# GpSimd's 16-point phases ahead of the third root, their sine in the silu stretch, and a forward slab's tables two places behind its first stage

## The chip, the cores and the metric

The kernel runs on one core of a Trainium2 chip. The metric is device time in microseconds (us) of one execution of the whole program, 204.77 us before the change (median of 3 runs, 204.67 to 204.78). Beside it stands a profile of one further execution. Engines are written as the profile writes them: PE is TensorE's matmul and PEld its weight load, DVE is VectorE, ACT is ScalarE, POOL is GpSimd, SP is SyncE, which issues the DMAs. Every engine works through its own instructions in the order in which the program wrote them.

## The reference

The input x is 2048 rows of 640 elements. It is normalised by row, and then takes two ways: a two-dimensional Fourier filter, and a gated feed-forward network whose output passes a silu. The two are multiplied and added to x.

```python
xn = _layernorm(x, axis=-1)
# spectral part, over both axes of (S, D) = (2048, 640)
X = rfft2(xn)
X = X * (w_r + 1j * w_i)
s = irfft2(X)                                   # to bfloat16
# feed-forward part, F = 1536
g = silu((gelu(xn @ w_gate) * (xn @ w_up)) @ w_down)
return x + s * g
```

## The kernel before

**The two ways.** The feed-forward network is what fills TensorE. It runs over four groups (g) of 512 rows. In a group, for each of twelve tiles of 128 features, a *half* of five matmuls gives the gate (`psg`, then a GELU `ge` on ScalarE) and another half gives the up projection (`psu`, then the product `uT` on VectorE, line 795). Then follow the down projections of the group's four slabs of 128 rows: each slab in three thirds of eight matmuls, in chains of twelve that end in a silu (`G`, line 819, groups 0 and 3) or in a tanh form of it (`th`, `G`, lines 822 and 823, groups 1 and 2). `psg` and `psu` have two PSUM buffers each.

The Fourier filter is done by matmuls with tables of sines that the kernel computes. Its forward part goes over 16 slabs, slab n1 holding the rows with index n1 modulo 16. `slab_S1` (the *first stage*) multiplies five folded chunks of the slab by the table `Tfwd` into `pz` and casts it on ScalarE to `GEN` (line 545; the buffer shares the tile GEN, and there are four such places). `slab_D` (the *tables*: the matmuls with `FT`) takes that cast through six matmuls into `pd`, casts it on ScalarE to `zd` (line 579, four buffers), and SyncE stores it to `ZDR` in two DMAs (line 582). Both stages draw `pz` and `pd` from one ring of two PSUM buffers. When all 16 slabs are stored, `load_B2` reads them back, turned, into B in ten DMAs; a middle part of 16-point transforms (`s2_in`, `s2_out`, tables MG, N1, N2) and an inverse part follow, between the pieces of groups 2 and 3 of the network.

**What is folded.** Ahead of a first stage VectorE normalises a slab (`norm`, line 205) and folds it, four slabs at a time: `fold_x`, `fold_a`, `fold_b` give the chunks f, and `fold_y` in three steps gives the last chunk y. Row statistics come from `stats`; `root` computes the reciprocal standard deviations of four slabs, an addition on VectorE and a power on GpSimd (line 199). The third such root of four, for slabs 8 to 11, is `root, 8, 4`.

**The 16-point tables.** MG is built from the sines of 128 small phases. `mg_iota` and `mg_phase1` prepare constants on GpSimd. `mg_phase2` computes the phases `vg` with eight small GpSimd instructions (line 378). `mg_mask` takes them modulo 2048 on VectorE (line 417). `mg_sin` is their sine on ScalarE (`sg`, line 421), and `mg_build` copies and signs them into MG and MJ on GpSimd. `mg_turn` transposes both by DMA at places 45 and 46. The table sines Tinv and FT are computed at place 22, right behind an instruction that brings in the Silu table.

**What sets the order.** The order is written out by hand. The list `back` holds the pieces of the network. The n-th of them is called *place* n here. Places 0 to 23 are group 0's halves, 24 to 35 its down thirds, 36 to 59 group 1's halves (even places gate, odd places up), 60 to 71 its down thirds. `put(p, ...)` appends a step to place p. The program writes each piece and then the steps put at its place, in the order of the `put` calls. So an item of place p stands behind the piece of place p on every engine that both use. Nothing is moved after that; an engine starts its next instruction when its inputs and buffers are ready.

For the forward slabs the list `FA` names the place of each first stage, and the tables stand one place behind:

```python
    FA = (30, 32, 33, 35, 37, 39, 40, 42, 44, 46, 48, 50, 54, 55, 57, 58)
    for n1 in range(NS):
        put(FA[n1] + 1, slab_D, n1)
        put(FA[n1], slab_S1, n1)
```

Where slab n's tables and slab n+1's first stage share a place, the tables come first. `load_B2` is put at place 60, the first `s2_in` at place 67.

Of the kernel before, what the change touches and what calls it, by code (L numbers as in the profile page):

```python
# [32 lines left out]
def kernel(  # L33
# [40 lines left out]
    with tc.manual_schedule():  # L74
        build(nc, locals())


def build(nc, env):
# [792 lines left out]
    def put(s, *item):  # L871
        plan[s].append(item)
# [22 lines left out]
    put(0, lists)  # L895
    put(13, mg_iota)
    put(13, mg_phase1)
    put(23, mg_phase2)
    for it in ((silu_table,), (tinv_sin, 0), (tinv_sin, 1), (ft_sin, 0)):
        put(22, *it)  # L900
    for q in range(4):
        put(23 + q, tfwd, q)
    put(28, ft_sin, 1)
    put(36, mg_mask)
    put(37, mg_sin)
    put(37, mg_build)
    for at, *items in (
            (17, (stats, 8)), (18, (stats, 9)), (20, (stats, 10)), (22, (stats, 11), (root, 8, 4)),
            (24, (fold_x, 0, 4, 0), (fold_x, 0, 4, 1)), (25, (fold_a, 0, 4, 0), (fold_a, 0, 4, 1)),
            (26, (fold_b, 0, 4, 0), (fold_b, 0, 4, 1)), (27, (fold_y, 0, 4, 0), (fold_y, 0, 4, 1), (fold_y, 0, 4, 2)),  # L910
            (28, (norm, 8)), (29, (fold_x, 4, 4, 0), (fold_x, 4, 4, 1)), (30, (fold_a, 4, 4, 0)),
            (31, (fold_a, 4, 4, 1), (fold_b, 4, 4, 0)), (32, (fold_b, 4, 4, 1), (fold_y, 4, 4, 0)),
            (33, (fold_y, 4, 4, 1), (fold_y, 4, 4, 2), (norm, 9)), (34, (norm, 10), (norm, 11)), (35, (stats, 12)),
            (36, (stats, 13)), (37, (fold_x, 8, 4, 0)), (38, (fold_x, 8, 4, 1), (fold_a, 8, 4, 0)),
            (39, (fold_a, 8, 4, 1)), (40, (fold_b, 8, 4, 0), (fold_b, 8, 4, 1)), (41, (fold_y, 8, 4, 0)),
            (42, (fold_y, 8, 4, 1), (fold_y, 8, 4, 2), (half_stats, 14, 0)), (43, (half_stats, 14, 1)),
            (44, (stats, 15), (root, 12, 4)), (46, (norm, 12), (norm, 13)),
            (47, (norm, 14), (norm, 15)), (48, (fold_x, 12, 4, 0), (fold_x, 12, 4, 1)),
            (49, (fold_a, 12, 4, 0)), (50, (fold_a, 12, 4, 1), (fold_b, 12, 4, 0)), (51, (fold_b, 12, 4, 1)),
            (52, (fold_y, 12, 4, 0), (fold_y, 12, 4, 1)), (53, (fold_y, 12, 4, 2))):  # L920
        for it in items:
            put(at, *it)
    F0 = 30
    TURN = 45
    FA = (30, 32, 33, 35, 37, 39, 40, 42, 44, 46, 48, 50, 54, 55, 57, 58)
    for n1 in range(NS):
        put(FA[n1] + 1, slab_D, n1)
        put(FA[n1], slab_S1, n1)
    z_end = F0 + 30
    for k in range(4):  # L930
# [87 lines left out]
```

## Time and profile before

| what | value |
|---|---|
| median of 3 runs | 204.77 us (204.67 to 204.78) |
| the profiled execution | 204.84 us |
| its span in the trace | 203.1 us |
| PE busy | 195.4 us, 96% of the span |
| DVE busy | 132.0 us, 65% |
| ACT busy | 125.7 us, 62% |
| POOL busy | 37.9 us, 19% |
| DMA, mean over the span | 160 GB/s |
| places 30 to 60, by the trace | 41.7 to 88.7 us |

The span is counted from the first to the last instruction; the execution's own time has 1.7 us around it. An engine's busy time is a union of its instructions as drawn, and the drawn end of a matmul is modelled: consecutive starts tell more than ends. A row of the timeline reads: start in us from the beginning of the span, duration, engine, line of the kernel, operation, out<-in, shapes, and in brackets the idle time before it with what ended it. Consecutive instructions of one kind are merged into one row (x5). A row of the waits reads: who waited, for whom, the sum in us, how often, the longest.

### The profile page before, as it was taken

How to read it: one execution, taken by the hardware profiler on the slowest of the kernel's cores; microseconds unless marked ns; L12 is line 12 of the kernel's file. 1: busy time of each engine (PE TensorE's matmuls, PEld its weight loads, DVE VectorE, ACT ScalarE, POOL GpSimd, SP SyncE). 2: the span in 40 equal slices, each digit the busy share in tenths (PEclk: the TensorE clock that was granted, in tenths of full speed). 3: DMA queues.
4: the chain of work that ended last, by engine and by line, in shares of the span. 5: the costliest groups of instructions: out<-in, count | busy, mean ns of one | idle time of the engine just before them, and what ended most of it. 6: DMA issues, size and time to landing. Idle time of an engine off the chain costs nothing.

```text
span 203.1 us, 4169 instructions
## 1 busy us (share of the span) xinstructions
PE 195.4 (96%) x1549; PEld 118.2 (58%) x1549; DVE 132.0 (65%) x320; ACT 125.7 (62%) x219; POOL 37.9 (19%) x62
## 2 busy tenths in 40 slices
PE   7989999999789999999999999999999999999993
PEld 5778854777345555566643434357765555556773
DVE  7876969799757696222666476433239787878573
ACT  2548657967996665742687778623564756476632
POOL 5427679994050200000000000000000000000000
PEclk9999999999999999999999999999999999999999
DMA  5999999455558628227963222239900507141612
GB/s 168 340 343 329 400 282 177 90 186 194 136 145 143 167 76 325 82 65 219 326 163 67 74 97 97 100 103 269 303 8 2 164 4 221 36 129 39 190 62 70
DMA packets 40325, 32.44 MB, mean 160 GB/s; under 512 B 15088, under 2 KB 38256, under 8 KB 40048
## 3 DMA queue, kind: packets, MB, share of 16 engines
q1 hardware_dynamic: 40304, 32.17, 56.1%
q8 instruction: 12, 0.20, 0.4%
q14 instruction: 9, 0.07, 0.1%
HBM read 19.03 MB, written 7.88 MB: 133 GB/s over the span
## 4 chain that ended last, share of the span: by engine, by line
PE 67%; ACT 1%; issue 1%; DVE 0%
PE psg L789 18%; PE psu L789 17%; PE psg L814 10%; PE psu L814 9%; PE pv L706 2%; PE pd L553 2%; PE pu L653 2%; PE px L626 2%; PE pd L574 2%; PE pz L543 1%; PE pd L557 1%; ACT GEN L545 0%; PE pd L576 0%; ACT G L819 0%; DVE Yall L764 0%
## 5 line engine op out<-in xcount | busy, mean ns | idle before, releaser
L789 PE MATMUL psu<-xnT,Wu 128*128 128x512 bf16 (+2 forms) x295 | 61.5, 339 | 0.5 <-DVE uT L795 0.3
L789 PE MATMUL psg<-xnT,Wg 128*128 128x512 bf16 (+2 forms) x295 | 61.5, 341 | 0.0
L795 DVE TENSOR_TENSOR uT<-psu,ge 128x512 bf16<-128x512 f32 (+2 forms) x59 | 34.4, 587 | 29.4 <-PE psu L789 20.5
L793 ACT ACTIVATE ge<-psg 128x512 bf16<-128x512 f32 (+2 forms) x59 | 30.5, 517 | 26.7 <-PE psg L789 24.8
L814 PEld LDWEIGHTS <-uT 128*128 128x128 bf16 x396 | 37.2, 98 | 14.0 <-issue 0.4
L789 PEld LDWEIGHTS <-Wu 128*128 128x128 bf16 x295 | 26.4, 98 | 22.1 <-issue 3.2
L789 PEld LDWEIGHTS <-Wg 128*128 128x128 bf16 x295 | 26.6, 99 | 20.8 <-issue 1.6
L814 PE MATMUL psg<-Wd,uT 128*128 128x320 bf16 (+1 forms) x204 | 30.5, 294 | 0.0
L814 PE MATMUL psu<-Wd,uT 128*128 128x320 bf16 (+1 forms) x192 | 29.0, 296 | 0.0
L638 DVE TENSOR_TENSOR X<-xs,W 128x972 bf16<-128x972 bf16 (+2 forms) x22 | 13.3, 648 | 10.2 <-ACT xs L634 9.3
L579 ACT CAST zd<-pd 128x660 bf16<-128x660 f32 x16 | 11.3, 708 | 6.0 <-PE pd L576 3.5
L183 DVE BATCH_NORM_STATS2 st<-X 128x6 f32<-128x320 bf16 x32 | 14.1, 479 | 0.3 <-DMA X<-in_A_x_dram 0.2
L708 ACT CAST W<-pv 128x640 bf16<-128x640 f32 x16 | 11.1, 695 | 5.0 <-PE pv L706 5.0
L731 ACT ACTIVATE W<-pd 128x960 bf16<-128x960 f32 (+2 forms) x14 | 10.0, 779 | 5.8 <-PE pd L557 5.5
L659 ACT CAST X<-pu 128x486 bf16<-128x486 f32 (+4 forms) x22 | 12.3, 558 | 0.4
L545 ACT CAST GEN<-pz 128x640 bf16<-128x640 f32 x16 | 11.1, 691 | 1.8 <-PE pz L543 1.8
L634 ACT CAST xs<-px 128x972 bf16<-128x972 f32 (+2 forms) x11 | 10.3, 937 | 2.9 <-PE px L626 2.9
L823 DVE SCALAR_TENSOR_TENSOR G<-th,psg 128x320 bf16<-128x320 f32 x8 | 3.9, 488 | 11.7 <-ACT th L822 11.7
L737 DVE TENSOR_TENSOR W<-W 128x960 bf16<-128x960 bf16 (+1 forms) x12 | 6.9, 598 | 4.1 <-ACT W L731 4.1
L764 DVE TENSOR_TENSOR Yall<-Yall,G 128x640 bf16<-128x640 bf16 (+3 forms) x19 | 8.2, 434 | 1.4 <-ACT G L819 1.1
L574 PE MATMUL pd<-FT,GEN 128*128 128x132 bf16 x64 | 6.6, 227 | 2.4 <-ACT GEN L545 2.2
L574 PEld LDWEIGHTS <-GEN 128*128 128x128 bf16 x64 | 4.0, 98 | 8.2 <-ACT GEN L545 8.0
(135 smaller groups left out, 214.4 us busy)
## 6 DMA issues: line engine op xcount, KB each, us to landing
W<-W SPq DMA_DIRECT2D x4, 642.0 KB, 3.5
ZDR<-zd SPq DMA_DIRECT2D x32, 80.2 KB, 2.6
xt<-in_A_x_dram SPq DMA_DIRECT2D x8, 320.0 KB, 3.7
UDR<-X SPq DMA_DIRECT2D x10, 240.8 KB, 2.5
out_dram<-Yall SPq DMA_DIRECT2D x14, 160.0 KB, 2.2
B<-ZDR SPq DMA_DIRECT2D x8, 240.8 KB, 4.5
W<-UDR SPq DMA_DIRECT2D x4, 481.5 KB, 6.5
X<-in_A_x_dram SPq DMA_DIRECT2D x3, 640.0 KB, 7.2
```

Of the source, the lines that this page charges most:

```text
L183: nc.vector.bn_stats(out=st[:, k, :], in_=X[:, n1, 320 * k:320 * k + 320])
L545: nc.scalar.copy(out=Zt[n1], in_=pz)
L574: nc.tensor.matmul(l_cols(pd[:, g % 2], g), lhsT=z[:, g, :], rhs=FT[:, g, :], start=True, stop=True)
L579: nc.scalar.copy(out=zd.rearrange("p c (q e) -> p c q e", e=10), in_=pd[:, :, 0:330].rearrange("p c (e q) -> p c q e", q=33))
L634: nc.scalar.copy(out=xs, in_=px[:, :, 0:n * w].rearrange("p k (h l) -> p k h l", l=w))
L638: nc.vector.tensor_tensor(out=pp[-1], in0=xs, in1=WT[:, :, h0:h0 + n, l0:l0 + w], op=ALU.mult)
L659: nc.scalar.copy(out=us[:, :, :, c0:c0 + (w + 1 - m) // 2], in_=pv[:, :, :, m:w:2])
L708: nc.scalar.copy(out=vs, in_=pv)
L789: nc.tensor.matmul(ps, lhsT=WT[:, c, t * P:(t + 1) * P], rhs=xnT[g][:, c, c0:c1_], start=(c == 0), stop=(c == 4))
L793: nc.scalar.activation(out=ges[t], in_=ps, func=ACT.Gelu_apprx_tanh)
L795: nc.vector.tensor_tensor(out=uT[g][:, t, c0:c1_], in0=ps, in1=ges[t], op=ALU.mult)
L814: nc.tensor.matmul(ph, lhsT=uT[g][:, t, j * P:(j + 1) * P], rhs=Wd[:, t, c0:c1_], start=(t == 0), stop=(t == NT - 1))
```

## The change

Three things are moved; no instruction is added or taken away by the code itself.

- `mg_phase2` goes from place 23 to place 13. On GpSimd the eight phases then stand ahead of the third root (put at 22). `mg_mask` goes from place 36 to 30, `mg_sin` and `mg_build` from 37 to 31, which is among group 0's down thirds with their silu.
- On VectorE the norm of slab 8 goes from place 28 to 33, and those of 9 to 11 are all put at 34; two folds of slabs 4 to 7 are put one place earlier, at 28 and 29.
- A slab's tables are put two places behind its first stage, or at the next slab's first stage where that is nearer. The first stages of slabs 10, 11, 12 and 14 are put one place earlier (47, 49, 53, 56), and `FA` gets a seventeenth entry, 60, for the tables of slab 15.

```diff
     put(13, mg_iota)
     put(13, mg_phase1)
-    put(23, mg_phase2)
+    put(13, mg_phase2)
...
-    put(36, mg_mask)
-    put(37, mg_sin)
-    put(37, mg_build)
+    put(30, mg_mask)
+    put(31, mg_sin)
+    put(31, mg_build)
...
-            (28, (norm, 8)), (29, (fold_x, 4, 4, 0), (fold_x, 4, 4, 1)), (30, (fold_a, 4, 4, 0)),
+            (28, (fold_x, 4, 4, 0)), (29, (fold_x, 4, 4, 1)), (30, (fold_a, 4, 4, 0)),
...
-            (33, (fold_y, 4, 4, 1), (fold_y, 4, 4, 2), (norm, 9)), (34, (norm, 10), (norm, 11)), (35, (stats, 12)),
+            (33, (fold_y, 4, 4, 1), (fold_y, 4, 4, 2), (norm, 8)), (34, (norm, 9), (norm, 10), (norm, 11)), (35, (stats, 12)),
...
-    FA = (30, 32, 33, 35, 37, 39, 40, 42, 44, 46, 48, 50, 54, 55, 57, 58)
+    FA = (30, 32, 33, 35, 37, 39, 40, 42, 44, 46, 47, 49, 53, 55, 56, 58, 60)
     for n1 in range(NS):
-        put(FA[n1] + 1, slab_D, n1)
+        put(min(FA[n1 + 1], FA[n1] + 2), slab_D, n1)
         put(FA[n1], slab_S1, n1)
```

Slab 12's first stage at place 53 stands behind the last step of its own `fold_y`, which is put at place 53 before and after the change.

## The prediction

> **What bounds the kernel now.** I read the page's first part, then TensorE's waits, then the timelines of TensorE, ScalarE, VectorE and GpSimd between 36 and 104 us, and last the DMA issues around 91 us.
>
> ```profile
> PE 195.4 (96%) x1549; PEld 118.2 (58%) x1549; DVE 132.0 (65%) x320; ACT 125.7 (62%) x219; POOL 37.9 (19%) x62
> ```
> ```profile
> PEld L574 <- ACT GEN L545: 8.0, 14, 2.3
> ...
> PE pd L574 <- ACT GEN L545: 2.2, 3, 1.8
> ```
> TensorE is the bound (96%), and nearly all it waits for outside the start is the cast GEN that stands between a forward slab's first stage and its tables.
>
> ```profile
> 51.61 1.28 ACT L793 ACT_TABLE_LOAD   x1
> ...
> 53.40 0.70 ACT L579 CAST zd<-pd 128x660 bf16<-128x660 f32 x1
> 54.12 1.28 ACT L421 ACT_TABLE_LOAD   x1
> 55.41 0.40 ACT L421 ACTIVATE sg<-vg,negpi 128x128 f32<-128x128 int32 x1
> 55.72 0.67 ACT L545 CAST GEN<-pz 128x640 bf16<-128x640 f32 x1
> 56.41 1.28 ACT L793 ACT_TABLE_LOAD   x1
> ```
> ```profile
> 53.39 1.24 PE L789 MATMUL psg<-xnT,Wg 128*128 128x512 bf16 x5
> 56.45 0.42 PE L574 MATMUL pd<-FT,GEN 128*128 128x132 bf16 x4 [1.81 <-ACT GEN L545]
> ...
> 77.02 1.24 PE L789 MATMUL psu<-xnT,Wu 128*128 128x512 bf16 x5
> ...
> 79.17 0.39 PE L543 MATMUL pz<-Tfwd,f 128*128 128x128 bf16 x4
> 79.44 0.23 PE L543 MATMUL pz<-Tfwd,y 128*128 128x128 bf16 x1
> ...
> 87.29 0.41 PE L574 MATMUL pd<-FT,GEN 128*128 128x132 bf16 x4 [0.22 <-ACT GEN L545]
> ```
> Columns are start, duration, engine, line. The largest hole is at 54.5 to 56.45: the sine sg stands ahead of GEN on ScalarE and costs a table load before it and another behind it.
>
> **What is lost now.** A drawn end overlaps the next start, so I go by starts. Undisturbed steps from the PE timeline: a half (five matmuls) 1.08 us (77.02 to 78.10), eight down matmuls 1.08, a first stage 0.28 (83.88 to 84.16), the tables 0.31 (85.24 to 85.55). What a start is late beyond these steps: slab 2's tables 0.20, slab 4's 1.98 (due 53.39+1.08, came 56.45), 5's 0.35, 6's 0.24, 7's to 11's 0.07 each (0.35), slab 12's first stage 0.06, 13's tables 0.20, 15's 0.39. Sum 3.77 us between places 30 and 60. From a first stage's start to its GEN are 0.48 us, and from GEN to the tables 0.74 (63.56 to 64.30): 1.22 with ScalarE free, while one place gives 0.28+1.08=1.36. So one place suffices alone and fails when ScalarE has a GELU (0.50 from start to start) or another slab's zd cast (0.60) in front.
>
> **The change part by part.**
>
> *Sine at place 31.* ScalarE loses two loads (2x1.29) and 0.31 of sine ahead of slab 4's GEN. At 34.92 one load serves Silu, the table sines and the G rows, so the sine needs none at place 31. Its 0.31 fall between the silu of 44.10 and the next, which comes 0.21 behind a down chain ending at 45.43: hidden if the mask is there. GELU's load at 51.61 stays.
>
> *GpSimd's phases ahead of the third root.*
> ```profile
> 36.60 1.04 POOL L199 TENSOR_TENSOR rst<-ve,mhalf 128x4 f32<-128x4 f32 x1
> 37.65 1.37 POOL L378 TENSOR_SCALAR vg<-kr,n1x,php 128x16 int32<-128x16 int32 x1
> ...
> 40.38 1.88 POOL L378 TENSOR_SCALAR vg<-kr,n1x,phm 128x16 int32<-128x16 int32 x1
> ...
> 46.15 1.88 POOL L378 TENSOR_SCALAR vg<-kr,n1x,phs 128x16 int32<-128x16 int32 x1
> ...
> 56.96 0.30 POOL L378 TENSOR_SCALAR MG<-sg,pb 128x32 bf16<-128x32 f32 x1
> ```
> ```profile
> 37.56 0.96 DVE L493 TENSOR_TENSOR GEN<-X 128x1536 bf16<-128x1536 bf16 x1 [1.29 <-ACT Tinv L339]
> ...
> 38.96 1.30 DVE L503 TENSOR_TENSOR GEN<-GEN 128x1024 bf16<-128x1024 bf16 x2
> ...
> 41.50 0.68 DVE L469 TENSOR_TENSOR GEN<-X 128x1024 bf16<-128x1024 bf16 x1
> ...
> 44.28 0.41 DVE L496 TENSOR_TENSOR GEN<-X 128x512 bf16<-128x512 bf16 x1
> ```
> GpSimd is late: work of places 13 and 23 runs through from 28 to 48 us, so the move only swaps the eight phases with the root. Now they run from 37.65 to 48.03, 1.3 us each; the mask, at place 30, comes up on VectorE when L496 ends, at 44.69 less the 0.36 of the norm that leaves: 44.33. Moved up by the root's 1.04 and no more, the phases would end at 46.99, and VectorE, then ScalarE, would wait 2.7 us. That is the upper end. The lower end is the cost of such a row with VectorE idle: 0.27 apart (56.69, 56.96, 57.22). I take a mixture, because the slow ones end just behind a seam between VectorE's folds: 39.02, 40.42, 42.26 and 42.84 against seams at 38.86, 40.26, 42.18 and 42.68. From 36.60 to 37.56 VectorE is idle: three or four phases pass there (0.96/0.27). The rest take the four seams and end at 42.84; should one be over, VectorE stops at 44.33 for the mask, and so lets it through by 44.5. The mask then costs nothing on TensorE. The page "SBUF — State Buffer" of the Trainium skill (section "Who interferes with whom") has it as a rule: a VectorE instruction with two SBUF inputs and a GpSimd one that reads SBUF exclude each other, and the second waits for the first to finish. The rows agree; without the rule one would take the 46.99, and the sum would be that of the first rival.
>
> The root then starts at 42.84 to 44.6; its first user, the norm of slab 8, now stands at place 33, at about 48.4, 3 us after the root even if it takes 1.04 behind a seam. The norm's 0.36 moves from before slab 4's folds to behind them: these are due at 53.1 and done by 48.9. SyncE's transpose of slab 8 waits for that norm, but is issued only at 52.82 now. The nine instructions that build MG fall among the folds: at 1.3 each they end by 58, and their transposes are issued at 71.61. No cost.
>
> *Tables two places behind, four first stages one place earlier.* Where two places lie between, 0.28+2x1.08+0.31 cover everything: the delays of slabs 2, 4, 6, 7, 8, 10, 11 and 15 go. Where first stages stand in adjoining places (32/33, 39/40, 46/47, 55/56) the tables keep one place, now with the previous slab's tables back to back ahead of the first stage. zd is then in front of GEN: slabs 1, 5 and 13 wait 0.2 (rows: slab 6 0.24, 13 0.20); slab 9, with a GELU in front as well, waits 0.39 as slab 15 does now. Sum 0.99.
>
> Slab 12's first stage moves from place 54 to 53, where the last fold of its y is issued behind place 53's own uT product. In the rows psu starts at 77.02, uT at 78.37, the fold at 78.97, and its result feeds TensorE at 79.44: 2.42 behind psu's start. TensorE gets to that fifth matmul at 1.08+0.22=1.30. New loss: 1.12.
>
> Each slab's two ZDR stores move with its tables. SyncE issues them at 0.6 each and stands in front of w loads and transposes there, with up to 2.4 us of lag (slab 11: cast at 76.14, issue at 79.26). The cast zd has four buffers and so needs the store of four slabs before: the tightest is slab 10's, landed at 82.98 behind the twin copy of W, for slab 14's cast at about 85. No cost.
>
> *Behind place 60.* Slab 15's tables now come after the first eight down matmuls of place 60, 1.08 nearer to the first matmul on B (96.39). In the DMA view the first two B loads landed at 94.15 and 94.81: 1.58 of slack, less 1.08, leaves 0.5. Queue order ahead of them on SyncE is the same. No cost; everything behind has the same order and moves along.
>
> **Sum.** Lost before 3.77; after 0.99+1.12=2.11. Gain 1.66. The profiled execution took 204.84 (span 203.1, 1.7 around it), 0.07 over the median of 204.77: 204.84-1.66=203.18, so 203.2.
>
> **Rivals.**
> 1. *The mask comes late (slower).* GpSimd's 1.3 us are its own and not VectorE's doing. Mask at 47.0, sine 47.25 to 47.56, silu 0.34, zd 0.60, GEN at 48.5, slab 1's tables at 49.24, where TensorE is ready at 47.13: 2.1 instead of 0.2, plus up to 0.3 later echoes: 203.18+1.9 to 2.2, about 205.2. It costs from a mask later than about 45.0 on and eats the gain at about 46.6. Against it: the seams, and 0.30 for such a row at 56.96. Chance 0.09.
> 2. *B becomes the wait.* With landings 0.5 to 1 us later than at 94.81, the first matmul on B waits up to 0.5: 203.7. The issue to landing of the B loads spreads from 2.7 to 6.6 us, but the long ones are the later ones of the burst. 0.08.
> 3. *VectorE falls behind.* In front of slab 12 its last fold but one now ends only about 0.1 before place 53's psu; TensorE has gained 1.6 us on it. If the folds or the fourth root are 0.3 to 0.9 later, slab 12 waits that much longer: 203.5 to 204.1. 0.13.
> 4. *Within 0.2% of before* (several such waits, or a mask near 46.5): 204.4 to 205.2. 0.10, of which nearly half below 204.5.
> 5. *More than forecast*: half of the small waits don't come: 202.5 to 202.7. 0.05.
>
> **Chances.** Forecast (202.7 to 203.7) 0.55; the rivals as given. 0.2% (0.4 us) is about what a measurement can tell from no change: faster 0.55+0.08+0.13+0.05 is 0.81, rounded to 0.80; same 0.10; slower 0.10. The range 202.6 to 204.5 leaves out rival 1, the upper part of 4 and the lowest of 5, some 0.19.
>
> **What would show it.** One ACT_TABLE_LOAD between 51 and 58 us, not three, and sg between two silu rows near 44.6; first vg rows near 0.3 us, the last ended by 44.5, and no VectorE gap over 0.3 ahead of L417; waits of tables on GEN down from 8.0 us at PEld to some 3 (the loads' view counts what is hidden too); one new hole of about 1.1 us before y's matmul of slab 12; no hole before the first px. Wrong it would be by a VectorE gap of 2 us at L417, or by slab 12 or px waiting longer than above.

## The result, and the profile after

The changed kernel takes 203.14 us (median of 4 runs, 203.03 to 203.26) against 204.74 us before (204.67 to 204.78, 4 runs on the same chip): 1.60 us less, a ratio of 0.9922 with a 95% interval of 0.9905 to 0.994. The prediction was 203.2 us, the sum's gain 1.66 us. The profiled execution took 203.26 us with a span of 201.5 us.

The page's first part of the changed kernel, and its waits (who waited for whom, sum in us, times, longest):

```profile
PE 193.4 (96%) x1534; PEld 118.6 (59%) x1549; DVE 132.2 (66%) x320; ACT 122.7 (61%) x217; POOL 37.4 (19%) x62
```
```profile
PEld L574 <- ACT GEN L545: 2.2, 4, 0.7
...
PEld L543 <- DVE y L479: 1.3, 2, 1.1
...
PE pz L543 <- DVE y L479: 1.0, 1, 1.0
```

ScalarE has two instructions and 3.0 us less: two table loads are gone. The weight loads of the tables wait on GEN in 4 places for 2.2 us, where it was 14 places and 8.0 us. The largest single wait between places 30 and 60 is now slab 12's for its y, 1.1 us. The other wait for y, 0.2 us, is slab 0's, and it was there before.

GpSimd's and VectorE's timelines of the changed kernel around the phases:

```profile
36.78 0.37 POOL L378 TENSOR_SCALAR vg<-kr,n1x,php 128x16 int32<-128x16 int32 x1
37.13 0.37 POOL L378 TENSOR_SCALAR vg<-kr,n1x,phs 128x16 int32<-128x16 int32 x1
37.46 0.37 POOL L378 TENSOR_SCALAR vg<-kr,n1x,phm 128x16 int32<-128x16 int32 x1
37.80 1.37 POOL L378 TENSOR_SCALAR vg<-kr,n1x,phs 128x16 int32<-128x16 int32 x1
...
42.95 1.61 POOL L378 TENSOR_SCALAR vg<-kr,n1x,phs 128x16 int32<-128x16 int32 x1
44.52 1.03 POOL L199 TENSOR_TENSOR rst<-ve,mhalf 128x4 f32<-128x4 f32 x1
```
```profile
37.71 0.96 DVE L493 TENSOR_TENSOR GEN<-X 128x1536 bf16<-128x1536 bf16 x1 [1.29 <-ACT Tinv L339]
...
44.60 0.23 DVE L417 TENSOR_SCALAR vg<-vg 128x128 int32<-128x128 int32 x1
44.74 1.29 DVE L503 TENSOR_TENSOR GEN<-GEN 128x1024 bf16<-128x1024 bf16 x2
```

Three phases pass 0.34 us apart while VectorE is idle. The fourth starts 0.09 us behind VectorE's first fold and takes 1.37. The last ends at 44.56, and the mask starts at 44.60, some 0.1 us behind the end of the instruction before it.

ScalarE and TensorE of the changed kernel:

```profile
44.86 0.40 ACT L421 ACTIVATE sg<-vg,negpi 128x128 f32<-128x128 int32 x1 [0.17 <-DVE vg L417]
45.78 0.44 ACT L819 ACTIVATE G<-psu 128x320 bf16<-128x320 f32 x1 [0.52 <-PE psu L814]
...
52.09 1.28 ACT L793 ACT_TABLE_LOAD   x1
```
```profile
67.92 0.42 PE L574 MATMUL pd<-FT,GEN 128*128 128x132 bf16 x4 [0.22 <-ACT GEN L545]
...
74.80 1.24 PE L789 MATMUL psu<-xnT,Wu 128*128 128x512 bf16 x5
75.88 0.39 PE L543 MATMUL pz<-Tfwd,f 128*128 128x128 bf16 x4
77.23 0.23 PE L543 MATMUL pz<-Tfwd,y 128*128 128x128 bf16 x1 [0.96 <-DVE y L479]
...
94.19 0.71 PE L814 MATMUL psu<-Wd,uT 128*128 128x320 bf16 x4
94.82 0.40 PE L626 MATMUL px<-B,MG 64*64 64x162 bf16 x5
```

The sine lies in a stretch in which ScalarE would have been idle and needs no load. Of the three loads between 51 and 58 us only GELU's is left, at 52.09. Slab 12's first four matmuls start when due, and the fifth comes 77.23-75.88 = 1.35 behind them instead of 0.22: 1.13 us lost. The first matmul on B is as late as before (0.09 us behind the down matmuls), and the second of B's first loads landed at 94.30, 0.52 us ahead of it.

### The profile page after: what moved, and what is told of

The parts are those of the page before. It is cut to its first block, busy times and chain, and to the rows that moved or that the text cites. A ratio compares the mean times of both kernels' runs of the same rounds, so it can differ in the third digit from the quotient of the medians.

```text
span 201.5 us, 4153 instructions
## 1 busy us (share of the span) xinstructions
PE 193.4 (96%) x1534; PEld 118.6 (59%) x1549; DVE 132.2 (66%) x320; ACT 122.7 (61%) x217; POOL 37.4 (19%) x62
## 4 chain that ended last, share of the span: by engine, by line
PE 64%; DVE 1%; issue 1%; ACT 0%; DVEq 0%
PE psu L789 16%; PE psg L789 16%; PE psg L814 10%; PE psu L814 10%; PE pv L706 2%; PE pd L553 2%; PE pu L653 2%; PE px L626 2%; PE pd L574 1%; PE pd L557 1%; PE pz L543 1%; DVE uT L795 0%; PE pd L576 0%; DVE y L479 0%; ACT G L819 0%
## 5 line engine op out<-in xcount | busy, mean ns | idle before, releaser
L789 PE MATMUL psg<-xnT,Wg 128*128 128x512 bf16 (+2 forms) x286 | 60.4, 338 | 0.8 <-ACT xnT L850 0.2
L199 POOL TENSOR_TENSOR rst<-ve,mhalf 128x1 f32<-128x1 f32 (+1 forms) x7 | 5.4, 767 | 23.0 <-DVE ve L197 23.0
L765 DVE TENSOR_TENSOR Yall<-Yall,xt 128x640 bf16<-128x640 bf16 (+3 forms) x19 | 8.3, 439 | 0.7
```

The costliest lines, as they stand in the source:

```text
L789: nc.tensor.matmul(ps, lhsT=WT[:, c, t * P:(t + 1) * P], rhs=xnT[g][:, c, c0:c1_], start=(c == 0), stop=(c == 4))
```

## The ledger of late starts

All runs are read in the way of the prediction: on TensorE, between slab 0's first stage and the first matmul on B, each start is compared with the start before it plus the undisturbed step. What is later than that is lost. A number alone, as in "5: 0.24", means that slab's tables; "12 y" is the fifth matmul of slab 12's first stage, read at the half behind it, which makes it up to 0.01 more than at its own start. The 0.19 to 0.28 us that slab 0's first stage waits for its own y at place 30, in all kernels but the last, and the 0.1 us ahead of the first matmul on B are left out. The last two columns are the change against before: of the ledger, and of the medians of runs on the same chip.

| kernel | late starts, us | sum | ledger | medians |
|---|---|---|---|---|
| before | 2: 0.19, 4: 1.97, 5: 0.35, 6: 0.24, 7 to 11: 0.08 each, 12 y: 0.06, 13: 0.20, 15: 0.38 | 3.79 | | |
| changed | 1: 0.22, 5: 0.24, 9: 0.38, 12 y: 1.14, 13: 0.20 | 2.18 | -1.61 | -1.60 |
| sine alone | 2: 0.19, 4: 0.28, 6: 0.38, 7 to 11: 0.08 each, 12 y: 0.06, 13: 0.20, 15: 0.39 | 1.90 | -1.89 | -1.90 |
| tables alone | 1: 0.22, 4: 1.22, 5: 1.43, 9: 0.38, 12 y: 1.14, 13: 0.20 | 4.59 | +0.80 | +0.64 |
| y at 52 | 1: 0.22, 5: 0.24, 9: 0.39, 12 y: 0.46, 13: 0.20 | 1.51 | -2.28 | -2.40 |
| root first | 1: 0.58, 5: 0.24, 9: 0.39, 12 y: 1.14, 13: 0.20 | 2.55 | -1.24 | -1.43 |
| first stages back | 1: 0.22, 5: 0.24, 12 y: 0.06, 14: 0.20 | 0.72 | -3.07 | -3.14 |
| always two | 12 y: 0.06 | 0.06 | -3.73 | -3.86 |
| last tables at 61 | as changed, and 0.78 at the first matmuls on B | 2.96 | -0.83 | -0.88 |
| always two, first at 31 | 12 y: 0.06 | 0.06 | -3.73 | -3.78 |

The ledger and the medians agree to 0.2 us. What comes before the ledger scatters by a little more: slab 0's first stage at place 30 started at 42.58 to 42.94 us in these profiles (43.67 in one, below), with the same program up to there but for small moves on GpSimd and VectorE.

## The experiments

**The two halves of the change.** The first kernel has the phases, mask, sine and norms of the changed kernel and the first stages and tables of before. The second has only the first stages and tables of the changed kernel. The norms and folds were not moved by themselves in any run. (Of the two folds that the section on the change names, only one moves, from place 29 to 28; the other stood at 29 already.)

```diff
 sine alone (against the changed kernel)
-    FA = (30, 32, 33, 35, 37, 39, 40, 42, 44, 46, 47, 49, 53, 55, 56, 58, 60)
+    FA = (30, 32, 33, 35, 37, 39, 40, 42, 44, 46, 48, 50, 54, 55, 57, 58)
-        put(min(FA[n1 + 1], FA[n1] + 2), slab_D, n1)
+        put(FA[n1] + 1, slab_D, n1)
```
```diff
 tables alone (against the kernel before)
-    FA = (30, 32, 33, 35, 37, 39, 40, 42, 44, 46, 48, 50, 54, 55, 57, 58)
+    FA = (30, 32, 33, 35, 37, 39, 40, 42, 44, 46, 47, 49, 53, 55, 56, 58, 60)
-        put(FA[n1] + 1, slab_D, n1)
+        put(min(FA[n1 + 1], FA[n1] + 2), slab_D, n1)
```

> The phases, mask, sine and norms as in the changed kernel, first stages and tables at the places of before (tables one place behind). Theory (what is lost on TensorE between places 30 and 60 adds up from small waits): slab 4's wait of 1.98 us falls to about 0.16, slab 5's 0.35 goes, the rest stays as before (slab 2 0.20, slab 6 0.24 to 0.37, slabs 7 to 11 0.07 each, slab 12 0.06, slab 13 0.20, slab 15 0.39): 1.6 to 1.7 us lost instead of 3.77, so 2.0 to 2.2 us faster than before, 202.6 to 202.8, and 0.3 to 0.5 us faster than the changed kernel. Rival (the sine pays only together with the later tables, or the tables are what pays): 203.1 or more.

Measured: 202.94 us (202.81 to 203.02) beside 204.84 before, ratio 0.9904 (0.9888 to 0.9919). TensorE at slab 4:

```profile
53.49 1.24 PE L789 MATMUL psg<-xnT,Wg 128*128 128x512 bf16 x5
54.84 0.42 PE L574 MATMUL pd<-FT,GEN 128*128 128x132 bf16 x4
```

The gain is 1.90 us, a little under the 2.0 to 2.2 expected: slab 4 still waits 0.28, not 0.16, and slab 6 the upper of its two values. The rival falls: the sine pays alone. The forecast lead over the changed kernel, 0.3 to 0.5 us, is 0.3 by the differences to before. The intervals of the two ratios overlap, so this lead rests on the ledger.

> First stages and tables at the places of the changed kernel, the phases, mask, sine (place 37, with its two table loads) and norms as before. Theory: slab 1 waits 0.2, slab 4 about 1.0 and slab 5 about 1.3 behind the two loads, slab 9 0.39, slab 12's y 1.12, slab 13 0.2: 4.2 us lost instead of 3.77, so 0.4 to 0.8 us slower than before, 205.1 to 205.5. Rival (two places cover the loads, and the move of the tables gains by itself): 203.5 to 204.3.

Measured: 205.48 us (205.37 to 205.62), ratio 1.0031 (1.0019 to 1.0042): 0.64 us slower than before, as the theory had it. ScalarE and TensorE of this kernel:

```profile
53.73 1.28 ACT L421 ACT_TABLE_LOAD   x1
55.02 0.40 ACT L421 ACTIVATE sg<-vg,negpi 128x128 f32<-128x128 int32 x1
55.33 0.69 ACT L579 CAST zd<-pd 128x660 bf16<-128x660 f32 x1
55.92 0.69 ACT L545 CAST GEN<-pz 128x640 bf16<-128x640 f32 x1
56.63 1.28 ACT L793 ACT_TABLE_LOAD   x1
```
```profile
56.67 0.42 PE L574 MATMUL pd<-FT,GEN 128*128 128x132 bf16 x4 [1.05 <-ACT GEN L545]
...
59.77 0.42 PE L574 MATMUL pd<-FT,GEN 128*128 128x132 bf16 x4 [1.27 <-ACT GEN L545]
```

Ahead of slab 4's GEN stand a load, the sine and a zd cast, 2.2 us from 53.73 to 55.92. Two places (2.16 us) don't cover that and the steps from GEN to the tables: slab 4's tables come 1.2 us late. The second load stands behind this GEN and ahead of slab 5's, whose tables have one place only and come 1.4 late. So the third part of the change, first stages and tables together, loses time on its own, and by the ledger also beside the sine: sine alone loses 1.90 us, both together 2.18.

**Slab 12's y.** The last fold of y for slabs 12 to 15 goes one place earlier, ahead of place 53's product uT.

```diff
-            (52, (fold_y, 12, 4, 0), (fold_y, 12, 4, 1)), (53, (fold_y, 12, 4, 2))):
+            (52, (fold_y, 12, 4, 0), (fold_y, 12, 4, 1), (fold_y, 12, 4, 2))):
```

> The changed kernel with the last fold of slabs 12 to 15's y one place earlier (52 instead of 53), so that it stands ahead of place 53's uT product on VectorE. Theory: the fold then starts behind the fold before it, near 76.07 in the changed kernel's trace, and y reaches TensorE near 76.55, due 76.10: the wait of 1.13 us falls to 0.45, 0.6 to 0.7 us faster than the changed kernel, 202.4 to 202.55. Rival (y is late for the folds behind it in the queue, not for the product ahead of it): no change, 203.1.

Measured: 202.44 us (202.35 to 202.76), ratio 0.9884 (0.9871 to 0.9898), as expected. VectorE of the changed kernel, then VectorE and TensorE of this one:

```profile
75.61 0.43 DVE L476 TENSOR_TENSOR y<-GEN 128x512 bf16<-128x512 bf16 x1
76.15 0.69 DVE L795 TENSOR_TENSOR uT<-psu,ge 128x512 bf16<-128x512 f32 x1
76.76 0.41 DVE L479 TENSOR_TENSOR y<-y,X 128x512 bf16<-128x512 bf16 x1
```

```profile
75.95 0.42 DVE L479 TENSOR_TENSOR y<-y,X 128x512 bf16<-128x512 bf16 x1
76.29 0.68 DVE L795 TENSOR_TENSOR uT<-psu,ge 128x512 bf16<-128x512 f32 x1
```
```profile
75.76 0.39 PE L543 MATMUL pz<-Tfwd,f 128*128 128x128 bf16 x4
76.43 0.23 PE L543 MATMUL pz<-Tfwd,y 128*128 128x128 bf16 x1 [0.29 <-DVE y L479]
```

The fold now ends at 76.37 and its matmul starts at 76.43, 0.45 late. So 0.68 us of the wait was queue order: a fold of 0.4 us stood behind a product that started 0.1 us behind the fold before and kept VectorE for 0.6. The 0.45 that stay are the folds themselves, which reach their last step only at 75.95.

**Why the phases were slow.** The phases go behind the third root again; mask and sine stay where the change put them.

```diff
-    put(13, mg_phase2)
+    put(23, mg_phase2)
```

> The changed kernel with the eight phases put behind the third root on GpSimd again (place 23); mask and sine stay at 30 and 31. Theory (GpSimd's phases are slow only while VectorE folds, one passing at each seam, and fast as soon as VectorE waits): the root takes the idle stretch up to 37.7, four phases pass at the seams up to 43.0, VectorE stops for the mask near 44.5 and the other four take 0.35 each: mask near 45.9, sine near 46.1, slab 1's tables wait 0.85 instead of 0.23, about 0.6 us slower than the changed kernel, 203.6 to 203.9. Rival (1.3 us a phase is GpSimd's own time): the last phase ends near 48.2 as before, slab 1's tables wait 3 us, 205.8 to 206.3.

Measured: 203.41 us (203.27 to 203.57), ratio 0.9929 (0.9915 to 0.9943). GpSimd and VectorE of this kernel:

```profile
36.37 1.04 POOL L199 TENSOR_TENSOR rst<-ve,mhalf 128x4 f32<-128x4 f32 x1
37.41 1.39 POOL L378 TENSOR_SCALAR vg<-kr,n1x,php 128x16 int32<-128x16 int32 x1
...
42.59 1.61 POOL L378 TENSOR_SCALAR vg<-kr,n1x,php 128x16 int32<-128x16 int32 x1
44.16 0.36 POOL L378 TENSOR_SCALAR vg<-kr,n1x,phs 128x16 int32<-128x16 int32 x1
44.49 0.36 POOL L378 TENSOR_SCALAR vg<-kr,n1x,phm 128x16 int32<-128x16 int32 x1
44.83 0.36 POOL L378 TENSOR_SCALAR vg<-kr,n1x,phs 128x16 int32<-128x16 int32 x1
```
```profile
45.22 0.23 DVE L417 TENSOR_SCALAR vg<-vg 128x128 int32<-128x128 int32 x1 [1.11 <-POOL vg L378]
```

Five phases take 0.6 to 1.9 us each while VectorE folds; from 44.1, where VectorE stops for the mask, three take 0.34 each. GpSimd's own time for a phase is therefore about a third of a microsecond, and the rival is out. The mask came at 45.2, earlier than the 45.9 expected, because this profile runs 0.4 us early and a fifth phase passed. The size was missed with it: slab 1's tables are 0.58 late, not 0.85, and 203.41 us lies below the 203.6 to 203.9 expected. The move on GpSimd is worth 0.36 us by the ledger (0.58 against 0.22); the medians show about 0.2, and the intervals of the two ratios overlap.

**Places of the first stages, and two places for all.** The third kernel of this group also moves slab 0's first stage to 31.

```diff
 first stages back (against the changed kernel)
-    FA = (30, 32, 33, 35, 37, 39, 40, 42, 44, 46, 47, 49, 53, 55, 56, 58, 60)
+    FA = (30, 32, 33, 35, 37, 39, 40, 42, 44, 46, 48, 50, 54, 55, 57, 58, 60)
```
```diff
 always two (against the changed kernel)
-    FA = (30, 32, 33, 35, 37, 39, 40, 42, 44, 46, 47, 49, 53, 55, 56, 58, 60)
+    FA = (30, 32, 33, 35, 37, 39, 40, 42, 44, 46, 48, 50, 54, 55, 57, 58)
-        put(min(FA[n1 + 1], FA[n1] + 2), slab_D, n1)
+        put(FA[n1] + 2, slab_D, n1)
```
```diff
 first at 31 (against "always two")
-    FA = (30, 32, 33, 35, 37, 39, 40, 42, 44, 46, 48, 50, 54, 55, 57, 58)
+    FA = (31, 32, 33, 35, 37, 39, 40, 42, 44, 46, 48, 50, 54, 55, 57, 58)
```

> The changed kernel with the first stages of slabs 10, 11, 12 and 14 back at 48, 50, 54 and 57 and the changed kernel's rule for the tables. Theory: slab 12's wait for y (1.14 us) falls to 0.06, slab 9's 0.38 goes (its tables get two places), slab 14's tables now wait 0.2 in place of slab 13's: 1.4 us faster than the changed kernel, 201.6 to 201.9. Rival (the first stages one place earlier are needed for B's loads or by later slabs): 202.5 or more.

> First stages at the places of before, each slab's tables always two places behind, also where the next first stage stands between. Theory: every wait of tables on GEN goes, 0.06 is left at slab 12: 2.0 to 2.2 us faster than the changed kernel, 201.0 to 201.3, 3.6 us under before. Rival (two first stages in a row make the ring of two PSUM buffers the wait): 201.6 or more, with waits of pz on zd or GEN.

> The kernel with tables always two places behind, and slab 0's first stage at place 31 instead of 30. Theory: its fifth matmul no longer waits 0.19 us for y of slab 0: 0.2 us faster than with place 30, 200.8 to 201.1. Rival: the three first stages then in adjoining places bring a new wait of as much, 201.0 to 201.3.

Measured: first stages back 201.64 us (201.56 to 201.83), ratio 0.9844 (0.983 to 0.9857), as expected. Always two 200.92 us (200.85 to 202.19), ratio 0.9822 (0.9797 to 0.9847), just under the 201.0 to 201.3 expected; one of its five runs took 202.19, the others at most 200.97, and nothing on record says why. With slab 0 at 31, 201.00 us (200.94 to 201.14), ratio 0.9812 (0.9799 to 0.9825). Before beside them 204.78. The first kernel differs from the changed one only in four first stages that stand one place later again: putting them one place earlier cost the change 1.5 us, and no run shows that it gained anything. TensorE's own waits over the whole of "always two":

```profile
PE psg L590 <- DVE negpi L213: 1.2, 1, 1.2
PE pt L849 <- DVE X L205: 1.0, 2, 0.7
PE psu L789 <- DVE uT L795: 0.3, 1, 0.3
...
```

No wait of the tables on GEN is left in its list, for TensorE or its weight loads, and none of `pz` on the PSUM ring: two first stages in a row do no harm. By the medians it is 3.9 us under before and 2.3 under the changed kernel. The last kernel can't be told from it: its profile shows slab 0's wait gone, but the 0.2 us it is worth is no more than the scatter of the start, and the medians differ by 0.08 the other way. These two are the fastest.

**The margin ahead of B.** Slab 15's tables and the issue of B's loads go one place later.

```diff
-    put(z_end, load_B2)
+    put(z_end + 1, load_B2)
...
-        put(min(FA[n1 + 1], FA[n1] + 2), slab_D, n1)
+        put(61 if n1 == NS - 1 else min(FA[n1 + 1], FA[n1] + 2), slab_D, n1)
```

(With it the last entry of `FA` becomes 61.)

> The changed kernel with slab 15's tables and the issue of B's loads at place 61 instead of 60. Theory: in the changed kernel the second of B's first two loads lands 0.52 us before the first matmul on B is due; another 1.08 turns that into a wait of about 0.56: 203.6 to 203.8. Rival (more slack than the landings show): 203.1 to 203.3. Rival (the slack is used up already): 204.2 or more.

Measured: 203.9 us (203.56 to 204.83, 10 runs), ratio 0.996 (0.9946 to 0.9974), so about 0.7 us over the changed kernel and 0.1 over the expected range. TensorE of this kernel:

```profile
94.91 0.71 PE L814 MATMUL psu<-Wd,uT 128*128 128x320 bf16 x4
95.80 0.36 PE L626 MATMUL px<-B,MG 64*64 64x162 bf16 x2 [0.18 <-DMA B<-ZDR]
96.33 0.40 PE L626 MATMUL px<-B,MG 64*64 64x486 bf16 x3 [0.16 <-DMA B<-ZDR]
96.66 1.26 PE L814 MATMUL psu<-Wd,uT 128*128 128x320 bf16 x8
```

From the down matmuls at 94.91 to those at 96.66 pass 1.75 us, where the changed kernel has 0.97 (94.19 to 95.16): 0.78 lost, expected 0.56. Most of the 0.22 between them is in the DMAs: from slab 15's tables to the landing of B's second load this profile has 7.65 us (88.63 to 96.28) and the changed kernel's 7.48 (86.82 to 94.30), 0.17 more. So the slack of about half a microsecond in the changed kernel is real, and the change used up all but that. This profile also holds a wait of 0.84 us for a load of Wu at 9.4 us, untouched by the edit, and its slab 0 starts at 43.67. The profiled run took 204.77 us, one other 204.83, and the remaining eight 203.56 to 204.05; whether the other slow one had the same wait is not shown.

## Why the prediction was right

- *The holes are waits for GEN, and the sine's loads are the largest.* Shown by "sine alone": slab 4's 1.97 becomes 0.28 and 1.9 us are gained, by the ledger more than by the whole change. Only the first of the two loads and the sine stood ahead of slab 4's GEN; the second load stood behind it.
- *The phases pass in VectorE's idle stretch and at its seams.* Three passed free, as forecast. Of the five slow ones four took the seams, and the one left over went through when VectorE stopped, ending at 44.56. The mask cost TensorE nothing. "Root first" shows the mechanism. The rule that the prediction cited from the page "SBUF — State Buffer" of the Trainium skill (section "Who interferes with whom") agrees with the rows of the phases, though not with that of the root (last section). The step of 0.27 that I took from the MG rows was 0.34 in fact.
- *Tables in adjoining places wait.* Forecast 0.2 for slabs 1, 5 and 13 and 0.39 for slab 9; measured 0.22, 0.24, 0.20 and 0.38. Together they are 1.04 us against 0.99. The other delays went.
- *Slab 12's y.* Forecast 1.12, measured 1.13 to 1.14, and "y at 52" shows its cause.
- *B's loads.* Forecast slack 0.5, measured 0.52, and "last tables at 61" shows that it is used up by the next place.
- *The sum.* 3.77 to 2.11 was forecast, 3.79 to 2.18 measured.

What was mis-sized did no harm: the MG instructions among the folds took 0.3 to 0.7 each and ended at 50.2, not 1.3 each to 58. The terms agree one by one, within 0.04 us, so that the sum isn't right by luck. What the prediction did not see is that the sine alone is ahead of the whole change: its own rows gave that (3.77 less slab 4's and 5's waits is 1.44, under 2.11), but it summed only the change as it stood.

## What to carry to other kernels

The time of an engine that is busy nearly throughout can be kept as a ledger: undisturbed steps from quiet rows, and each start's lateness beside them. Here it gave the difference of nine kernels to before within 0.2 us. Price a move at the place where it lands, in every queue: the ledger stood at 3.8 us before the edit and at 2.2 after, half of that because one first stage landed behind an instruction of its own place. In this kernel a distance of two places between first stage and tables was worth keeping without exception: each exception cost 0.2 to 0.4 us, and the buffers sufficed. It did not hide a table load and the sine ("tables alone").

## What the runs showed of the hardware

GpSimd's power for the root took 1.03 us (44.52 to 45.55) while VectorE's fold of 44.74 ran beside it at its usual pace (1.29 us for two), although the small scalar instructions before and after had to wait for seams. The profiles of five further kernels show the same 1.03 and 1.29; in a sixth, "first stages back", the power began at 44.04, 0.3 us before the end of a fold, and took 1.21. So not every GpSimd instruction is held up by folds, or holds them up, for its whole length. By the rule of the page "SBUF — State Buffer" of the Trainium skill (section "Who interferes with whom") one of the two should have waited; the measurement decides, and nothing was run to tell why they did not. In "root first" a queue of phases held up at 0.6 to 1.9 us apiece fell to 0.34 as soon as VectorE stopped. VectorE's wait for GpSimd was 1.1 us for that reason; at 0.6 to 1.9 us apiece the three phases left would have taken longer.
